# Two feed-forward layers after pooled attention: pairs of tiles 384 to 512 columns wide, first V remainders pooled on VectorE, and a new plan

## The chip, the cores and the metric

The kernel runs on one core of a Trainium2 chip. The metric is device time in microseconds (us) of one execution, the median of several. Engines are named as in the profile: PE multiplies matrices (TensorE), DVE is VectorE, ACT is ScalarE, POOL is GpSimd, and SP issues the DMA transfers.

## The reference

Attention over keys and values that are averaged in groups of 8, for 8 batches of 8 heads with 576 positions and 64 dimensions; then two feed-forward layers, 512 to 2048 to 512, over the 4608 tokens. All in float32.

```python
k_p = k.reshape(B, H, Sp, pool, D).mean(axis=3)      # 576 -> 72 positions
v_p = v.reshape(B, H, Sp, pool, D).mean(axis=3)
scores = scale * np.matmul(q, k_p.transpose(0, 1, 3, 2))
attn = softmax(scores)
x = np.matmul(attn, v_p)                             # then heads side by side: 4608 x 512
h = x @ moe_w_in;  x = np.maximum(0.01 * h, h) @ moe_w_out
h = x @ moe2_w_in; x = h * np.clip(h + 3.0, 0.0, 6.0) / 6.0 @ moe2_w_out
```

## The kernel before, in words

**Precision.** Each float32 operand of a large product is split into a high part in the matmul type (`float32r`) and the rest, and three products are summed (high x high, high x rest, rest x high). So each tile needs an ACT copy (the high part) and a DVE subtraction (the rest) before PE can use it.

**Attention** is done in 24 units (8 batches, three units each: two with 384 positions of four heads, one with the remaining 192 of all eight). `prep_k` and `prep_v` pool K and V; `scores`, `transposes`, `transpose_rem` and `values` follow. 72 pooled positions are kept as 64, the main part, and 8, the remainder. In the first batch, units 0 and 1 have V pooled by PE: `pool_v` (L427) multiplies eight slices by the identity into PSUM, once for the main part (128x128) and once for the remainder (32x64). Later units pool V by `sum_pool` (L405), a DVE reduction. DVE then multiplies the remainder by a mask (L486).

**The first 896 tokens** go through the first layer as plain tiles: 384 tokens with half of the hidden columns, then 512 tokens, then the 384 again with the other half (`moe_tile`; multiplications at L898 to L900 and L942 to L944). While these run, weights are loaded, decoded and split by ACT and DVE, and sums of weight blocks are stored in DRAM (`left`).

**Pairs.** The other 3712 tokens of the first layer (class `Pair1`) and all 4608 of the second (class `Pair`) go through as pairs of two tiles of n columns: four pairs, then five. A pair replaces the eight block products of a 2 x 2 product by seven (Strassen's scheme), in `first` and in `second`. `prepare` loads the pair's tokens (`xt`), forms the seven sums and splits them. Each pair streams all seven products' weights from `left` by SP's queue: 56 parts of 512 KB or fewer of 1 MB. Per pair `first` and `second` issue 336 multiplications each, all from `left_right` (L1163), whatever n is. n was 464, but 448 in the first pair of the second layer.

**The order of the work.** `C` holds slots at which attention units (`att`, `gaps`), weight sums (`left1`, `left2`, `when1`) and the next pair's preparation (`prep`, `prep2`) are recorded between the steps of the layers. The class `Plan` takes all recorded tasks with their dependencies and a price for each (`pe_cost`, `act_cost`, `dve_cost`, bytes over a rate), places them in time on every engine by list scheduling in 12 rounds, and the instructions are issued in that order, each engine first in, first out. Copies recorded early may go to ACT or DVE, as the planner finds. `Plan.order` also puts small multiplications of zeros (the fills, L1659) into PE's order where PE is planned to wait before the first layer's second multiplication begins, and twelve of them in a stretch of short multiplications and transposes (`weak`).

Of the kernel before, what the change touches and what calls it, by code (L numbers as in the profile page):

```python
# [10 lines left out]
F32 = mybir.dt.float32  # L11
# [8 lines left out]
B, H, S, D = 8, 8, 576, 64  # L20
DM, DFF = 512, 2048
POOL, SP = 8, 72
# [5 lines left out]
WIDTH = 464  # L28
STARTS = [0, T0, *range(T0 + T1, B * S + 1, WIDTH)]

# [3 lines left out]
    soon={0: 0, 1: 0, 2: 2000},  # L34
# [5 lines left out]
    when0=[0, 1, 0, 2, 5, 3, 10],  # L40
    att0=[0, 4, 8],
    gaps0=[0, 0, 2, 2, 0],
    when1=[4, 10, 20, 26],
    att1=[0, 7, 14, 22],
    gaps1=[0, 3, 3, 3, 0],
    att2=[0, 5],
    gaps2=[0, 1, 5, 6, 0],
    prep2=[26, 68],
    att=[[4, 26, 42, 51], [10, 24, 39, 58, 70], [0, 21, 40, 55], []],
    gaps=[[0, 7, 7, 11, 2], [0, 11, 9, 19, 1], [0, 2, 10, 11, 6], [7, 14, 2, 4, 4]],  # L50
    prep=[[85, 106], [94, 89], [102, 89], [84, 93]],
    left1=[[(0, 65)], [(1, 0), (2, 1), (3, 16)]],
    left2=[[], [], [(0, 40)], [(1, 23), (2, 45)], [(3, 18), (4, 39)], [(5, 23), (6, 40)], [(7, 15)]],
# [5 lines left out]
FIRST_LOADS = 1.35  # L59
WARM_FROM = 2700  # L60
# [47 lines left out]
class Plan:  # L108
# [102 lines left out]
    def order(self):  # L211
# [28 lines left out]
        out, busy, weak = [], WARM_FROM, 0.0  # L240
        for i in sorted(range(n), key=lambda i: (self.starts[i], i)):
            engine, cost, emit = self.chosen[i]
            if engine == "pe" and busy is not None:
                gap = self.starts[i] - busy
                out += [self.fill] * (int((gap - 200) / 56) + (6 if gap > 300 and busy > 12000 else 0))
# [13 lines left out]
def attention_moe_moe(ctx: ExitStack, tc: tile.TileContext, qt, kt, vm, vr, wt, wq, eye, mask, out):  # L259
# [42 lines left out]
    def pe_cost(n):  # L302
        return max(0.4435 * n + 5, 111)
# [124 lines left out]
    def pool_v(u):  # L428

        ps = buf("h", [128, 512], F32, 2, psum)  # L430
        u.vs, u.rs = ps("v", lambda t: t[:, 0:128]), ps("r", lambda t: t[:32, 128:192])
        for src, dst, n in ((u.v, u.vs, 128), (u.r, u.rs, 64)):

            def emit(src=src, dst=dst, n=n):
                for i in range(POOL):
                    PE.matmul(
                        out=dst.ap(),
                        lhsT=ident.ap()[: dst.ap().shape[0], : dst.ap().shape[0]],
                        rhs=src.ap()[:, i * n : i * n + n],
                        start=i == 0,  # L440
                        stop=i == POOL - 1,
                    )

            on_pe(1740 if n == 128 else 1320, emit, [src, ident], [dst], n < 128)
# [19 lines left out]
    def prep_v(u):  # L464
# [3 lines left out]
        if u.early:  # L468
            pool_v(u)
        else:  # L470
            sum_pool(u.vs, u.v, 128)
            sum_pool(u.rs, u.r, 64)
# [1157 lines left out]
    n = 11  # L1630
# [82 lines left out]
```

## Time and profile before

| | us |
|---|---|
| median of 3 runs | 1557.65 |
| the three runs | 1557.65, 1560.13, 1549.45 |
| the profiled execution | 1553.07 |
| its span, first to last instruction | 1551.3 |

The profile's page gives each engine's busy time in the span; the views of the trace split it by stretch (windows), by instruction in order of time (timeline), by what an engine waited for (waits), and by the chain of work that ended last. Times in the views are counted from the span's start. The granted clock is TensorE's, where 1.00 is 2.4 GHz and 0.50 is 1.2 GHz. The two halves of the first pair begin at 236.2 and 316.8 us, the following pairs at 391.2, 552.1 and 709.2, the second layer's at 849.8 us.

### The profile page before, as it was taken

The page shows a single profiled execution, that of the slowest core. Times are in us where ns is not written, and L with a number is a line of the kernel's source. Part 1 is how long each engine was busy: PE and PEld are TensorE (multiplying, and loading weights), DVE is VectorE, ACT ScalarE, POOL GpSimd, SP SyncE. Part 2 cuts the span into 40 slices and gives each one's busy share as a digit, 9 for nine tenths or more (in the row PEclk, how much of TensorE's full clock was granted, in tenths as well). Part 3 has the DMA queues.
Part 4 walks back from the last instruction along what each step waited for, and adds up shares of the span by engine and source line. Part 5 has one row for each costly group of instructions (what it writes and reads, how often), then busy time and mean ns, then how long its engine had stood idle before and what let it go on. Part 6 is the DMA issues. An engine that isn't in the chain of part 4 may idle for free.

```text
span 1551.3 us, 23074 instructions
## 1 busy us (share of the span) xinstructions
PE 1543.8 (100%) x7905; PEld 1381.0 (89%) x7905; DVE 1195.2 (77%) x2124; ACT 997.9 (64%) x2267; POOL 2.9 (0%) x14
## 2 busy tenths in 40 slices
PE   9999999999999999999999999999999999999999
PEld 7988898899989888888888999988888888888888
DVE  7999998599769876897597769559756946885494
ACT  5988767767777677766666656455555644664454
POOL 0000000000000000000000000000000000000000
PEclk9999999999999999999999999999999999999999
DMA  7999779998999899999997987766866775676664
GB/s 265 342 366 324 265 279 347 323 311 302 327 325 332 269 312 331 307 327 324 326 342 257 343 277 251 264 208 226 289 218 216 254 252 206 228 259 222 213 234 145
DMA packets 141140, 434.65 MB, mean 280 GB/s; under 512 B 14432, under 2 KB 56032, under 8 KB 122848
## 3 DMA queue, kind: packets, MB, share of 16 engines
q1 hardware_dynamic: 141024, 433.18, 80.7%
q8 instruction: 63, 1.03, 0.3%
q14 instruction: 53, 0.43, 0.1%
HBM read 345.57 MB, written 87.56 MB: 279 GB/s over the span
## 4 chain that ended last, share of the span: by engine, by line
PE 87%; DVE 7%; ACT 3%; DMA 1%; issue 1%; SPq 0%; ACTq 0%; DVEq 0%
PE y L1163 42%; PE h L1163 23%; PE a L1163 13%; PE a L715 2%; DVE raw L1028 2%; PE a L520 1%; DVE gl L329 1%; DVE st L329 1%; DMA xh<-x 1%; DVE w L1028 1%; PE h L898 1%; PE h L900 1%; PE h L899 1%; ACT s L604 1%; PE a L664 1%
## 5 line engine op out<-in xcount | busy, mean ns | idle before, releaser
L1028 DVE TENSOR_TENSOR w<-y,w 128x464 f32<-128x464 f32 (+1 forms) x124 | 79.2, 639 | 116.7 <-PE y L1163 113.5
L322 ACT ACTIVATE gh<-w 128x464 fp32r<-128x464 f32 (+1 forms) x140 | 82.5, 590 | 65.4 <-PE y L1163 31.1
L1163 PE MATMUL y<-w,xh 128*128 128x464 f32 (+1 forms) x552 | 122.8, 372 | 0.0
L1028 DVE TENSOR_TENSOR w<-w 128x464 f32<-128x464 f32 (+1 forms) x184 | 113.6, 639 | 3.2 <-ACT w L916 2.8
L1163 PEld LDWEIGHTS y<-w,xh 128*128 128x128 f32 x552 | 103.2, 188 | 11.2
L1361 DVE SCALAR_TENSOR_TENSOR gl<-w,gh 128x464 fp32r<-128x464 f32 (+1 forms) x140 | 89.0, 639 | 22.9 <-ACT gh L322 22.7
L319 ACT CAST gh<-w 128x464 fp32r<-128x464 f32 x128 | 74.3, 582 | 43.8 <-PE y L1163 22.2
L329 DVE TENSOR_TENSOR gl<-w,gh 128x464 fp32r<-128x464 f32 x128 | 81.6, 641 | 14.7 <-ACT gh L319 14.2
L1163 PE MATMUL y<-w,xl 128*128 128x464 f32 (+1 forms) x408 | 91.7, 373 | 0.0
L1332 ACT ACTIVATE gh<-w,three 128x464 f32<-128x464 f32 (+1 forms) x60 | 40.9, 681 | 69.8 <-DVE w L1028 69.8
L1163 PEld LDWEIGHTS y<-w,xl 128*128 128x128 f32 x408 | 76.1, 188 | 8.4
L1028 DVE TENSOR_TENSOR w<-h,w 128x464 f32<-128x464 f32 (+1 forms) x52 | 33.3, 640 | 62.7 <-PE h L1163 62.5
L916 ACT ACTIVATE w<-w 128x464 f32<-128x464 f32 x96 | 57.1, 601 | 36.5 <-DVE w L1028 35.5
L319 ACT COPY w<-y 128x464 f32<-128x464 f32 (+2 forms) x105 | 57.0, 546 | 32.4 <-PE y L1163 31.6
L329 DVE TENSOR_TENSOR st<-raw,st 128x512 fp32r<-128x512 f32 x88 | 60.4, 688 | 18.5 <-ACT st L319 18.2
L329 DVE TENSOR_TENSOR w<-x,w 128x464 fp32r<-128x464 f32 (+1 forms) x96 | 60.2, 639 | 11.6 <-ACT w L319 11.6
L1163 PE MATMUL y<-gh,raw 128*128 128x464 f32 (+1 forms) x224 | 69.1, 369 | 0.0
L1163 PE MATMUL h<-w,xl 128*128 128x464 f32 (+1 forms) x300 | 67.8, 373 | 0.0
L604 ACT ACTIVATE s<-a,mx 128x72 f32<-128x72 f32 x204 | 62.2, 339 | 7.4 <-DVE mx L580 7.1
L1163 PE MATMUL y<-w,w 128*128 128x464 f32 x288 | 64.4, 373 | 0.0
L1163 PE MATMUL h<-w,xh 128*128 128x464 f32 (+1 forms) x288 | 64.4, 372 | 0.0
L322 ACT ACTIVATE sb<-w 128x464 fp32r<-128x464 f32 (+1 forms) x70 | 41.3, 590 | 34.4 <-PE y L1163 16.6
(296 smaller groups left out, 4264.8 us busy)
## 6 DMA issues: line engine op xcount, KB each, us to landing
raw<-left SPq DMA_DIRECT2D x60, 1024.0 KB, 4.9
xl<-left SPq DMA_DIRECT2D x90, 512.0 KB, 5.3
left<-st SPq DMA_DIRECT2D x176, 256.0 KB, 5.5
xh<-left SPq DMA_DIRECT2D x86, 512.0 KB, 5.7
w<-left SPq DMA_DIRECT2D x74, 512.0 KB, 5.6
xh<-left SPq DMA_DIRECT2D x33, 1024.0 KB, 4.8
xl<-left SPq DMA_DIRECT2D x25, 1024.0 KB, 4.9
raw<-wq SPq DMA_DIRECT2D x16, 1024.0 KB, 7.5
```

What stands on the lines that cost most here:

```text
L319: a = lambda: ACT.copy(out=dst.ap(), in_=src.ap())
L322: a = lambda: ACT.mul(out=dst.ap(), in_=src.ap(), mul=scale)
L329: lambda: DVE.tensor_tensor(out=dst.ap(), in0=a.ap(), in1=f32(b.ap()), op=ALU.subtract),
L520: PE.matmul(out=to.get()[:, 2 * SP * i : 2 * SP * i + 2 * SP], lhsT=u.q.ap()[:, pi * HALF + CQ * c : pi * HALF + CQ * c + CQ], rhs=keys[u. ...
L604: ACT.activation(out=at()[:, c, h, :], in_=ps.get()[:, o : o + SP], func=AF.Exp, bias=mx.get()[:, c, h : h + 1], accum_out=sm.get()[:, 4 * ...
L664: PE.transpose(out=placed(u, ps.get(), c), in_=u.p(c, pi), identity=ident.ap())
L715: PE.matmul(out=ps.get()[:, c0 : c0 + n], lhsT=l(), rhs=r.ap()[:, c0 : c0 + n], start=i == 0, stop=i == len(ops) - 1)
L916: lambda: ACT.activation(out=dst.ap(), in_=src.ap(), func=AF.Prelu, alpha=0.01),
L1028: on_dve(n, lambda: DVE.tensor_tensor(out=dst.ap(), in0=a.ap(), in1=b.ap(), op=op), [a, b], [dst])
L1163: PE.matmul(out=o, lhsT=l, rhs=r, start=first and i == m == 0, stop=last and i == len(left) - 1 and m == 2, skip_group_check=True,)
L1332: lambda: ACT.activation(out=r.ap(), in_=h.ap(), func=AF.Relu, bias=three.ap()),
L1361: lambda: DVE.scalar_tensor_tensor(out=lo.ap(), in0=v.ap(), scalar=1.0 / 6.0, in1=f32(hi.ap()), op0=ALU.mult, op1=ALU.subtract),
```

## The change

- **Widths.** `WIDTHS1` and `WIDTHS2` replace one width: the first layer's four pairs are 384, 512, 448, 512 wide, the second layer's five are 512, 512, 512, 384, 384. Where a pair's columns come from two tiles of the layer before, `load_x` issues one transfer for each.
- **V remainders.** `pool_v` keeps only the main part on PE; the remainder of units 0 and 1 is reduced by DVE like all others, and the host lays it out for that.
- **Prices of the plan.** `pe_cost` is n/2.4 + 14 ns for multiples of 128, else + 16; the first loads count 1.08 instead of 1.35 of their bytes, the first weight loads 1.4; the fills at the start are counted from 980 ns at 107 ns each, later ones at 56, in gaps less 100 ns instead of 200.
- **Slots.** Nearly all slots of `C` are new, and the second layer's preparation has a pair of its own (`prep3`, 66 and 109 instead of 80 and 96). The count of operations per unit and per pair stays.

```diff
-WIDTH = 464
-STARTS = [0, T0, *range(T0 + T1, B * S + 1, WIDTH)]
+WIDTHS1 = [384, 512, 448, 512]
+WIDTHS2 = [512, 512, 512, 384, 384]
+STARTS = [0, T0, *(T0 + T1 + sum(WIDTHS1[: i // 2]) * 2 + (WIDTHS1[i // 2] if i % 2 else 0) for i in range(8)), B * S]
...
-    soon={0: 0, 1: 0, 2: 2000},
+    soon={0: 0, 1: 0, 2: 2000, 4: 0, 3: 0, 5: 0},
...
-    att=[[4, 26, 42, 51], [10, 24, 39, 58, 70], [0, 21, 40, 55], []],
+    att=[[4, 26, 33, 50], [10, 24, 39, 58, 75], [0, 21, 46, 58], []],
...
-FIRST_LOADS = 1.35
-WARM_FROM = 2700
+FIRST_LOADS = 1.08
+FIRST_WEIGHTS = 1.4
+WARM_FROM = 980
...
-                out += [self.fill] * (int((gap - 200) / 56) + (6 if gap > 300 and busy > 12000 else 0))
+                out += [self.fill] * (int((gap - 100) / (56 if out_of_rest else 107)) + (6 if gap > 300 and busy > 12000 else 0))
+                out_of_rest = True
...
     def pe_cost(n):
-        return max(0.4435 * n + 5, 111)
+        return max(n / 2.4 + (14 if n % 128 == 0 else 16), 111)
...
     def pool_v(u):
-        ps = buf("h", [128, 512], F32, 2, psum)
-        u.vs, u.rs = ps("v", lambda t: t[:, 0:128]), ps("r", lambda t: t[:32, 128:192])
-        for src, dst, n in ((u.v, u.vs, 128), (u.r, u.rs, 64)):
...
-            on_pe(1740 if n == 128 else 1320, emit, [src, ident], [dst], n < 128)
+        u.vs = buf("h", [128, 512], F32, 2, psum)(None, lambda t: t[:, 0:128])
...
+        on_pe(1800, emit, [u.v, ident], [u.vs])
...
             pool_v(u)
         else:
             sum_pool(u.vs, u.v, 128)
-            sum_pool(u.rs, u.r, 64)
+        sum_pool(u.rs, u.r, 64)
...
-    widths = [448] + [WIDTH] * 4
-    pairs1 = [Pair1(T0 + T1 + 2 * WIDTH * i, WIDTH) for i in range(4)]
-    pairs = [Pair(2 * sum(widths[:i]), n) for i, n in enumerate(widths)]
+    pairs1 = [Pair1(STARTS[2 + 2 * i], n) for i, n in enumerate(WIDTHS1)]
+    pairs = [Pair(2 * sum(WIDTHS2[:i]), n) for i, n in enumerate(WIDTHS2)]
...
-        prepare_pair(p.jobs, nxt, (80, 96))
+        prepare_pair(p.jobs, nxt, C["prep3"])
```

What this does to the order of instructions is shown at three places; lines below 1000 move by up to four. In PE's order the fills of the opening were 57 at the start and then groups of 17, 2, 9, 1, 12, 12 and 19; they are 41 and then 13, 13, 18, 12, 19, 12, 2, 12, 17 and 20. Before, only the last group stood behind the first multiplication with weights; now the last four do.

VectorE in the opening, from the second half of unit 1's key pooling to the mask of unit 0's V remainder. Before (`h_230` is PE's PSUM tile of pooled V):

```order
L409 TENSOR_REDUCE w_1_96<-w_1_96 128x72
L589 TENSOR_TENSOR sb_244<-y_1_207,mx_219 128x3x144
L615 TENSOR_SCALAR inv_248<-sm_211 128x12
L616 RECIPROCAL inv_248<-inv_248 128x12
L622 TENSOR_TENSOR rn_257<-s_198,inv_248 128x96
L638 TENSOR_TENSOR s_198<-s_198,inv_248 128x768
L580 TENSOR_REDUCE mx_219<-y_1_253 128x3x2
L486 TENSOR_TENSOR w_1_103<-h_230,mask_240 32x256
```

The same stretch of VectorE after (`raw_157` holds the loaded V of unit 0):

```order
L413 TENSOR_REDUCE w_1_96<-w_1_96 128x72
L594 TENSOR_REDUCE sm_203<-s_177 128x3x2
L327 TENSOR_SCALAR keys_1_79<-w_1_96 64x72 x2
L578 TENSOR_REDUCE mx_217<-y_1_198 128x3x2
L613 TENSOR_SCALAR inv_246<-sm_203 128x12
L413 TENSOR_REDUCE raw_157<-raw_157 32x64
L614 RECIPROCAL inv_246<-inv_246 128x12
L587 TENSOR_TENSOR sb_252<-y_1_198,mx_217 128x3x144
L620 TENSOR_TENSOR rn_254<-s_177,inv_246 128x96
L484 TENSOR_TENSOR w_1_149<-raw_157,mask_210 32x256
```

The reduction of the remainder (32x64) now stands in VectorE's queue, the mask reads its result instead of PSUM, and the scaling of `s` and the last maximum come behind the mask; the scaled keys of unit 1's second half are VectorE's too.

PE where the first layer begins, before (`h_342` is pooled V of unit 1, `h_434` the first product with weights, `y_3` the values of unit 1):

```order
L436 MATMUL h_342<-w_1_294,ident_168 32x64 x8
L898 MATMUL h_434<-xh_324,w_1_327 128x384
L899 MATMUL h_434<-xl_329,w_1_327 128x384
L900 MATMUL h_434<-xh_324,w_1_327 128x384
L898 MATMUL h_434<-xh_324,w_1_327 128x384
L899 MATMUL h_434<-xl_329,w_1_327 128x384
L900 MATMUL h_434<-xh_324,w_1_327 128x384
L715 MATMUL y_3_446<-w_1_83 128x384
```

The same place of PE after:

```order
L662 MATMUL y_2_409<-ident_153,sb_252 128x128 x3
L662 MATMUL y_2_416<-ident_153,sb_252 128x128 x3
L896 MATMUL h_421<-xh_333,w_1_341 128x384
L897 MATMUL h_421<-xl_339,w_1_341 128x384
L898 MATMUL h_421<-xh_333,w_1_341 128x384
L896 MATMUL h_421<-xh_333,w_1_341 128x384
L897 MATMUL h_421<-xl_339,w_1_341 128x384
L898 MATMUL h_421<-xh_333,w_1_341 128x384
L713 MATMUL y_3_433<-w_1_84 128x384
```

The pooling of the remainder is gone from PE, and the transposes of unit 1 (`y_2`), which stood ahead of the third unit's scores, now stand behind them.

SP's queue in the opening, before (`w_1_294` is V of unit 1; `w_1_242`, `w_1_259`, `w_1_278`, `w_2_419` and `w_2_456` are weights; `w_2_456` takes the buffer that held `w_1_294`):

```order
L797 DMA w_1_278<-wt 128x1024
L336 DMA w_1_294<-vm 128x1024
L336 DMA w_1_103<-qt 128x768
L797 DMA w_1_242<-wt 128x1024
L336 DMA w_1_294<-vr 32x512
L336 DMA raw_354<-kt 128x1152
L797 DMA w_1_278<-wt 128x1024
L336 DMA raw_397<-vr 32x512
L797 DMA w_2_419<-wt 128x1024
L797 DMA w_1_259<-wt 128x1024
L797 DMA w_2_456<-wt 128x1024 x2
```

SP's queue after (`w_1_262` is V of unit 1, and `w_2_444` takes its buffer):

```order
L340 DMA w_1_262<-vm 128x1024
L340 DMA w_1_262<-vr 32x512
L795 DMA w_1_297<-wt 128x1024
L340 DMA w_1_149<-qt 128x768
L795 DMA w_1_212<-wt 128x1024
L340 DMA raw_358<-kt 128x1152
L795 DMA w_1_297<-wt 128x1024
L795 DMA w_2_414<-wt 128x1024
L795 DMA w_2_444<-wt 128x1024
L340 DMA raw_450<-vr 32x512
```

V of unit 1 is loaded one weight transfer earlier, its remainder right behind it, and the first transfer into its buffer stands ahead of two of those that it stood behind.

## Rows read from the trace of the kernel before

**Rows 1.** The page's busy times: us, share of the span, instructions, by engine.
```profile
PE 1543.8 (100%) x7905; PEld 1381.0 (89%) x7905; DVE 1195.2 (77%) x2124; ACT 997.9 (64%) x2267; POOL 2.9 (0%) x14
```
**Rows 2.** PE's waits: what it waited for, us in total, times, longest.
```profile
PE a L715 <- DVE w L320: 1.2, 1, 1.2
...
PE a L664 <- DVE s L638: 0.4, 1, 0.4
PE a L715 <- ACT tr L319: 0.3, 1, 0.3
```
**Rows 3.** Windows: stretch, length, busy us by engine, granted clock, DMA share, GB/s.
```profile
60.00:140.00 80.00, 79.93 (x430) 68.22 (x429) 78.76 (x151) 68.26 (x202) 0.00 (x0) 1.00 1.01 358
...
236.20:391.20 155.00, 155.00 (x801) 139.13 (x800) 125.14 (x225) 110.12 (x281) 0.40 (x2) 1.00 0.93 319
391.20:552.10 160.90, 160.90 (x867) 144.71 (x865) 129.62 (x233) 117.17 (x315) 0.00 (x0) 1.00 0.93 315
552.10:709.20 157.10, 156.60 (x820) 139.80 (x814) 126.94 (x230) 116.58 (x304) 0.00 (x0) 1.00 0.93 317
709.20:849.80 140.60, 140.60 (x674) 126.01 (x673) 104.81 (x180) 89.73 (x165) 0.00 (x0) 1.00 0.91 316
```
**Rows 4.** The chain that ended last, in the pairs: start us, us, what.
```profile
339.81 10.03 PE h L1163 x48
...
947.21 9.73 PE a L1163 x48
```
**Rows 5.** PE's timeline in the plain tiles: start us, us, instruction.
```profile
50.11 0.33 PE L942 MATMUL y<-gh,w 128*128 128x384 f32 x1
...
58.26 0.34 PE L944 MATMUL y<-gh,w 128*128 128x384 f32 x1
...
127.83 0.39 PE L898 MATMUL h<-xh,w 128*128 128x512 f32 x1
...
134.41 0.39 PE L900 MATMUL h<-xh,w 128*128 128x512 f32 x1
```
**Rows 6.** VectorE's groups by shape: count, busy us, mean ns, idle before.
```profile
L1028 DVE TENSOR_TENSOR w<-y,w 128x464 f32<-128x464 f32 x112 | 71.7, 640 | 101.6 <-PE y L1163 98.4 <-ACT w L916 1.3 <-ACT gh L1332 1.0
...
L409 DVE TENSOR_REDUCE raw<-raw 32x64 f32<-32x512 f32 x14 | 9.3, 666 | 0.0
...
L329 DVE TENSOR_TENSOR gl<-u,gh 128x384 fp32r<-128x384 f32 x16 | 8.8, 551 | 0.4 <-ACT gh L319 0.4
```
**Rows 7.** The chain that ended last, in the opening.
```profile
0.98 5.95 PE idle L1659 x57
...
14.01 1.80 PE h L436 x16
...
18.33 4.77 PE a L715 x8
...
23.85 3.32 PE h L436 x16
...
30.07 1.00 PE h L436 x16
...
32.32 3.16 PE y L715 x8
...
36.73 1.07 PE idle L1659 x19
...
42.03 3.96 PE a L715 x16
```
**Rows 8.** ScalarE's timeline in the opening.
```profile
4.39 0.26 ACT L322 ACTIVATE keys<-raw 64x72 f32<-64x72 f32 x1 [2.16 <-DVE raw L409]
```
**Rows 9.** Windows of PE alone: stretch, length, busy us, granted clock, DMA share, GB/s.
```profile
18.00:20.00 2.00, 1.67 (x5) 1.00 1.04 404
...
21.00:26.00 5.00, 5.00 (x18) 0.50 0.65 245
```
**Rows 10.** SP's timeline in the opening.
```profile
16.69 15.22 SPq L797 DMA_DIRECT2D w<-wt  x4
```

More of the change, by code (lines that the diff above doesn't have):

```diff
@@ L39 @@
     parts=31,
-    when0=[0, 1, 0, 2, 5, 3, 10],
+    when0=[0, 0, 2, 0, 4, 0, 5],
     att0=[0, 4, 8],
[L42 to L45, printed above, removed]
+    gaps0=[0, 0, 2, 2, 4],
+    when1=[4, 8, 21, 26],
+    att1=[0, 4, 14, 22],
+    gaps1=[0, 3, 0, 3, 1],
     att2=[0, 5],
-    gaps2=[0, 1, 5, 6, 0],
-    prep2=[26, 68],
-    att=[[4, 26, 42, 51], [10, 24, 39, 58, 70], [0, 21, 40, 55], []],
[L50 to L53, printed above, removed]
+    gaps2=[0, 1, 5, 6, 3],
+    prep2=[33, 72],
+    att=[[4, 26, 33, 50], [10, 24, 39, 58, 75], [0, 21, 46, 58], []],
+    gaps=[[0, 6, 7, 11, 0], [0, 11, 9, 16, 3], [0, 0, 10, 11, 13], [29, 25, 3, 2, 32]],
+    prep3=[66, 109],
+    prep=[[82, 93], [98, 118], [95, 94], [98, 81]],
+    left1=[[[0, 66]], [[1, 14], [2, 6], [3, 19]]],
+    left2=[[], [], [[0, 32]], [[1, 42], [2, 41]], [[3, 16], [4, 37]], [[5, 9], [6, 42]], [[7, 5]]],
 )
@@ L239, in order @@
         self.idle = []
-        out, busy, weak = [], WARM_FROM, 0.0
+        out, busy, weak, out_of_rest = [], WARM_FROM, 0.0, False
         for i in sorted(range(n), key=lambda i: (self.starts[i], i)):
@@ L428, in pool_v, with emit @@
     def pool_v(u):
-        ps = buf("h", [128, 512], F32, 2, psum)
-        u.vs, u.rs = ps("v", lambda t: t[:, 0:128]), ps("r", lambda t: t[:32, 128:192])
-        for src, dst, n in ((u.v, u.vs, 128), (u.r, u.rs, 64)):
[L434 to L442, printed above, removed]
-            on_pe(1740 if n == 128 else 1320, emit, [src, ident], [dst], n < 128)
+        u.vs = buf("h", [128, 512], F32, 2, psum)(None, lambda t: t[:, 0:128])
+        def emit():
+            for i in range(POOL):
+                PE.matmul(
+                    out=u.vs.ap(), lhsT=ident.ap(), rhs=u.v.ap()[:, i * 128 : i * 128 + 128], start=i == 0, stop=i == POOL - 1
+                )
+        on_pe(1800, emit, [u.v, ident], [u.vs])
     held_keys, held_values, whole_v, whole_r = {}, {}, {}, {}
@@ L795, in load_w @@
             on_dma(
-                1 << 20 if h is None else 1 << 19,
+                (1 << 20 if h is None else 1 << 19) * (FIRST_WEIGHTS if f == 0 else 1),
                 lambda dst=dst, cut=cut: DMA.dma_start(out=dst.ap().bitcast(I32), in_=cut(wt[ORDER[f]].bitcast(I32))),
@@ L1687 @@
     vm, vr = c(vm).reshape(B, 2, 128, 128, POOL), vr.reshape(B, 2, 32, D, POOL)
-    vm[0], vr[0] = [a[0].swapaxes(2, 3).reshape(a[0].shape) for a in (vm, vr)]
+    vm[0] = vm[0].swapaxes(2, 3).reshape(vm[0].shape)
     wi = moe_w_in.reshape(4, 128, NF, 128).transpose(2, 1, 0, 3).reshape(NF, 128, 512)
```

## The prediction

> **What bounds the kernel now.** I read the page's busy times first, then PE's waits, then one window per stage, then the chain of waits in the opening, then the timeline for the spacing of matrix multiplications. PE is busy for 1543.8 us of a 1551.3 us span [rows 1], and the view of waits has next to nothing after the opening: five waits before 31 us, in sum 2.4, the longest of 1.2; the third row here stands for three of 0.2 to 0.3 us [rows 2]. The windows say where other engines come close: VectorE is busy 78.76 of 80 us from 60 to 140 us, but PE has no gap there; in the four pairs of the first feed-forward layer (236.2 to 849.8 us) PE has no gap worth 1 us either, with the DMA engines at a share of 0.91 to 0.93 [rows 3]. So from about 31 us on the end is set by the sum of PE's multiplications, and before that by a chain through several engines. Only two things can shorten the kernel much: fewer ns per column in the long part, and a shorter opening.
>
> **Widths: a term of the long part.** Each of the nine pairs issues 336 multiplications in `first` and 336 in `second`, whatever its width; the tokens per layer stay 3712 and 4608. So the number of multiplications and of columns is the same, and what can differ is the time that a multiplication takes above its columns at 2.4 GHz. The chain gives 10.03 us for 48 of 464 columns (208.96 ns, 15.6 above 464/2.4) and 9.73 for 48 of 448 (202.7 ns, 16.0 above) [rows 4]. The other two widths run in the earlier tiles. At 384 the multiplication that starts at 58.26 is the 47th after the one at 50.11: 8.15/47 = 173.4 ns, 13.4 above 160. At 512, from 127.83 to 134.41 in 29 steps: 226.9 ns, 13.6 above 213.3 [rows 5]. Before, eight pairs are 464 wide and one 448; after, three are 384, five 512, one 448. Leaving out the 448 (672 x 202.7 both times): before 5376 x 0.20896 = 1123.4 us; after 2016 x 0.1734 + 3360 x 0.2269 = 349.6 + 762.4 = 1112.0. **Term: -11.4 us.** It lies wholly on the path, because PE is the bound there. The bounds: with the overheads of all widths equal it is 0; with a reading error of 0.01 us over 29 steps it is 1.2 us more or less.
>
> The Trainium skill's page TensorE: Matmul & The Clock Gate, section "Wait — 56ns, not 53.3ns?", puts the excess of a back-to-back multiplication at a fixed 2.5 ns, whatever its width. By that rule this term is 0, as count and columns stay; by the rows it is -11.4, and the rows decide, since they show 13 to 16 ns and a difference between widths.
>
> **The narrow pairs.** A 384-wide pair takes PE 672 x 0.1734 = 116.5 us instead of 140.4, but streams the same weights (29.4 MB). I added the bytes in SP's order from one pair's first weight stream to the next one's: before 47.6, 50.2, 50.6, 44.6 MB in the four pairs of the first layer, now 42.9, 54.2, 49.4, 46.5 MB, so the new slots take work out of the narrow first pair. The attention inside these stages is what the window is longer than 140.4 us: 14.6, 20.5, 16.7 and 0.2 us [rows 3]. New stage lengths: 131.1, 173.0, 152.9, 152.7 us, needing 327, 313, 323, 304 GB/s. The windows show 315 to 319 GB/s in these stages without a wait of PE, and 358 GB/s over 80 us from 60 to 140 us [rows 3]; so 327 is between what was given here and what was given at most. If 319 were the limit, the first pair would wait 42.9/0.319 - 131.1 = 3.4 us; if 358, 0. The nearest row by kind is the 319, but with its share at 0.93 it is not at its end; I take **+0.5 us**, bounds 0 and 3.4. VectorE: an operation of 464 columns takes 640 ns and one of 384 takes 551 [rows 6], a ratio of 0.86 against PE's 0.83. The fourth pair (without attention) has 104.8 us of VectorE, the first 125.1 [rows 3]; 104.8 x 0.86 + 20.3 = 110 of 131.1 us, so VectorE still hides behind PE; without that cover each operation more would cost 0.55 us. The last two 384-wide pairs have no attention and no weight preparation, and I cost them, the moved preparation slots, `soon` and the planner's new prices at nothing: they only order what lies beside PE's unbroken row of multiplications, and a slip would show as single waits of 0.2 to 0.8 us.
>
> **The opening.** I count what PE does up to the values of the third attention unit (42.03 in the chain) beside its real work.
> - Fills at the start (by the order of both programs): 57 take 5.95 us, 0.104 each [rows 7], and after only 41 stand there: -1.7 us. ScalarE's half of the first keys was done at 4.65 [rows 8], before the 41 fills can end (5.3); if the queries land later than that, part is waited for instead: bounds -1.7 and -0.5.
> - V remainders: PE's eight instructions of 32x64 take 1.00 us at 30.07 in the chain [rows 7]; the other eight run in a stretch padded with fills and cost nothing. VectorE gets two reductions of 0.67 us [rows 6], into a queue on which the first values wait. Term -1.0, bounds -2.0 and +0.3.
> - The clock: it was granted 0.50 from about 20 to 27 us, after a stretch (18 to 20) in which PE was busy 1.67 of 2 us [rows 9]. Eight multiplications of values took 4.77 us there and 3.16 at 32.32; sixteen of the V pooling took 3.32 and before 1.80 [rows 7]: 1.61 + 1.52 = 3.1 us lost. After, 12 and 19 fills stand around the transposes ahead of the values. Term -3.1, bounds -3.1 and 0.
> - Other fills: 72 before, 138 after, up to the point where PE runs unbroken; 19 take 1.07 us [rows 7], so 66 x 0.056 = +3.7. They stand where PE would wait, and the five waits of 2.4 us should mostly go [rows 2]: +1.3, bounds 0 and +3.7.
>
> Together **-4.5 us**; all ends to one side -6.8 and +3.5. What is late next: VectorE's queue, which I find filled from 7 us on.
>
> **Sum.** -11.4 + 0.5 - 4.5 = -15.4 us. The profiled execution took 1553.07 us, so 1537.7 by it. It lies 4.6 below the median of the three runs, which range over 10.7 us; the mean of these four executions is 1555.1, and from it I get 1539.7: I say **1540**. A measurement of this kernel can tell about 1%, 15.6 us, from no change; the forecast sits at that edge.
>
> **Rivals.**
> - A, the time above the columns doesn't depend on the width where a pair runs (the differences seen are those of other tiles: other weights, other buffers). Then the widths give 0 and the rest -4.0: 1551. For it: 384 and 512 were never run in a pair. Against: 448 and 464, both in pairs, agree with each other at 16, and the two multiples of 128 agree at 13.5 in two different tiles.
> - B, the clock falls again in the opening, as fills don't make it certain: -12.3, so 1543. For it: transposes and short multiplications still fill that stretch, and VectorE still ends the waits.
> - C, the slower one: the weight stream. SP's queue is first in, first out, and if the DMA engines give no more than a fixed rate in the first layer's pairs, every stage takes its bytes over that rate. At 310 GB/s the waits are 7.2, 1.9, 6.3 and 0, in sum 15.4: all is eaten; below, the kernel is slower than before. At 300 GB/s: 11.8 + 7.7 + 11.6 + 2.2 = 33.3 us, so -15.9 + 33.3 = +17.4: 1572. Against: 315 to 319 GB/s was given without one wait.
> - D, the opening gives more, all terms at their good ends: -11.4 - 6.8 = -18.2, so 1537. For it: four weight loads stood in SP's queue from 16.69 to 31.9 [rows 10], the third and fourth of them behind a buffer that PE's remainder pooling freed last; now it is freed after the main pooling and VectorE's reduction. Against: from 60 to 140 us PE had no gap to lose [rows 3].
>
> **How the numbers follow.** Forecast 0.50, A 0.08, B 0.22, C 0.05, D 0.15. Faster by over 1%: half of the forecast, most of D, a little of B (run-to-run spread): 0.43. Slower by over 1%: the worse half of C: 0.03. Within: 0.54. Range: D with the runs' spread below gives 1530; A with it, and C up to break-even, gives 1553.
>
> **What would show it.** Right: 48 multiplications of 512 and 384 columns in a pair take 10.89 and 8.32 us in the chain; PE's waits stay below 1 us each after 60 us; the granted clock stays at 1.00 from 15 to 30 us; the first values start near 16 to 17 us instead of 18.33 and those of the third unit near 37 instead of 42.03. Wrong: 512 at 229 ns or more (A); 0.50 in the opening (B); PE waiting for tiles streamed from `left` in the first 384-wide pair, or the DMA share at 1.0 through it (C); new fills between weights multiplications that PE had no need of.

## The result and the profile after

| | before | after |
|---|---|---|
| median, us | 1557.33 (6 runs, 1549.45 to 1560.13) | 1542.51 (6 runs, 1541.80 to 1544.41) |
| the profiled execution | 1553.07 | 1541.80 |
| its span | 1551.3 | 1540.0 |
| start of the first pair | 236.2 | 231.9 |
| from there to PE's last multiplication | 1311.0 | 1304.3 |

The ratio after to before is 0.9916, with a 95% interval of 0.9889 to 0.9943. The prediction said 1540 (1530 to 1553). The two profiled executions differ by 11.3 us of span: 4.3 up to the first pair, 6.7 in the nine pairs, 0.3 behind them.

Busy times of the page of the kernel after, which answer to [rows 1]:

```profile
PE 1529.5 (99%) x7923; PEld 1351.7 (88%) x7923; DVE 1196.0 (78%) x2123; ACT 997.2 (65%) x2270; POOL 2.9 (0%) x14
```

PE is busy 14.3 us less in a span that is 11.3 shorter: 3 us more of it are idle. The view of PE's waits in the kernel after (what it waited for, us in total, times, longest) shows where; it answers to [rows 2]:

```profile
PE a L662 <- DVE s L636: 2.1, 1, 2.1
...
PE y L941 <- DVE gl L333: 0.8, 1, 0.8
PE h L1161 <- ACT gh L323: 0.7, 1, 0.7
PE a L518 <- DMA q<-qt: 0.5, 1, 0.5
PE y L1161 <- DMA xh<-left: 0.5, 1, 0.5
PE h L1161 <- DVE gl L333: 0.4, 1, 0.4
```

Only at the place of the second row, near 230 us, did the kernel before wait too (0.3 us); the other five are new at their places. The largest is for the softmax scaling of the fifth attention unit (L636), at 67 us.

**The pairs.** The windows of the five stretches (four pairs of the first layer, then the second layer), with the instructions of `left_right` alone: stretch, length, PE's and its weight loads' busy us (count), granted clock, DMA share, GB/s. First before, then after:

```profile
236.20:391.20 155.00, 144.76 (x672) 125.36 (x673) 1.00 0.93 319
391.20:552.10 160.90, 146.27 (x674) 124.74 (x672) 1.00 0.93 315
552.10:709.20 157.10, 145.09 (x673) 124.77 (x674) 1.00 0.93 317
709.20:849.80 140.60, 140.60 (x674) 126.01 (x673) 1.00 0.91 316
849.80:1547.20 697.40, 697.40 (x3360) 630.80 (x3359) 1.00 0.69 240
sum 1311.00, PE 1274.11 PEld 1131.67; mean PE 254.82 PEld 226.33
```

```profile
231.90:364.40 132.50, 120.83 (x672) 116.21 (x673) 1.00 0.95 334
364.40:540.70 176.30, 159.21 (x675) 124.61 (x673) 1.00 0.90 316
540.70:692.30 151.60, 140.78 (x672) 125.12 (x673) 1.00 0.92 321
692.30:844.70 152.40, 152.40 (x674) 126.20 (x674) 1.00 0.90 304
844.70:1536.20 691.50, 690.62 (x3361) 610.93 (x3359) 1.00 0.70 241
sum 1304.30, PE 1263.84 PEld 1103.08; mean PE 252.77 PEld 220.62
```

The same number of multiplications takes 1274.11 us before and 1263.84 after: -10.3. The first, 384-wide stage got 334 GB/s, more than any of the four before. Multiplications of other tiles fill the rest of each stage; PE's busy time over all instructions is 1310.50 of 1311.0 us before and 1301.98 of 1304.3 after, so the other work in the pairs grew from 36.4 to 38.1 us, and the idle time from 0.5 to 2.3.

The growth of 1.7 us is no new work. One attention unit's last stage on PE (six transposes, three of the remainder, twelve multiplications of values) stands from 230.1 to 236.2 us before, ahead of the first pair, and from 233.1 to 237.2 us after, behind the start of the first pair. The transposes by themselves (L664 before, L662 after) in the windows of the pairs, the same columns as above:

```profile
236.20:1547.20 1311.00, 10.16 (x72) 8.64 (x72) 1.00 0.80 276
...
231.90:1536.20 1304.30, 11.44 (x78) 9.60 (x78) 1.00 0.80 277
```

So 1.7 of the 4.3 us by which the first pair starts earlier are work that was moved behind its start; at equal work the opening won 2.6.

The spacing itself, from the chain of the kernel after (start us, us, what), beside [rows 4]:

```profile
330.21 8.32 PE y L1161 x48
...
653.56 9.73 PE y L1161 x48
```

8.32/48 is 173.3 ns for 384 columns, and 9.73/48 is 202.7 for 448. A pair of 512 in the second layer reads 10.88 for 48, 226.7 ns ("1259.99 10.88 PE a L1161 x48"). The spacings foretold from plain tiles hold in the pairs.

**The opening.** The chain of the kernel after, beside [rows 7]:

```profile
6.62 0.73 PE idle L1656 x13
...
16.25 3.22 PE a L713 x8
19.47 1.98 PE h L438 x16
...
25.74 3.16 PE y L713 x8
...
68.29 0.88 DVE s L636
69.17 0.14 issue
69.30 1.46 PE a L662 x6
70.76 0.32 PE h L896
```

The first values start at 16.25 instead of 18.33 and take 3.22 instead of 4.77; the second values start at 25.74 instead of 32.32; those of the third unit at 35.97 instead of 42.03. So 6.1 us were won by then; 2.6 are left at the first pair (4.3, less the 1.7 of work moved behind its start), so 3.5 were given back. The last four rows show where: PE waits until 69.17 for VectorE (2.1 us in the list of waits), and the multiplication behind it takes 0.32 us where 384 columns take 0.17. Windows of the kernel after, around that place (PE, weight loads, DVE, ACT, POOL busy; granted clock; DMA share; GB/s):

```profile
21.00:26.00 5.00, 5.00 (x66) 4.38 (x64) 4.57 (x9) 4.33 (x15) 0.00 (x0) 1.00 0.78 251
...
67.00:69.00 2.00, 0.24 (x2) 0.00 (x0) 2.00 (x6) 1.98 (x6) 0.00 (x0) 1.00 1.09 383
...
70.00:72.00 2.00, 2.00 (x9) 2.00 (x8) 1.97 (x4) 1.97 (x5) 0.00 (x0) 0.50 1.18 283
```

From 21 to 26 us, where [rows 9] had 0.50, the clock is granted in full. PE then idles for most of 67 to 69 while VectorE and ScalarE are busy throughout, and from 70 to 72 the clock is 0.50.

### The profile page after: what moved, and what is told of

Its sections match the earlier page's. It is cut to its first block, busy times and chain, and to the rows that moved or that the text cites. A ratio compares the mean times of both kernels' runs of the same rounds, so it can differ in the third digit from the quotient of the medians.

```text
span 1540.0 us, 23125 instructions
## 1 busy us (share of the span) xinstructions
PE 1529.5 (99%) x7923; PEld 1351.7 (88%) x7923; DVE 1196.0 (78%) x2123; ACT 997.2 (65%) x2270; POOL 2.9 (0%) x14
## 4 chain that ended last, share of the span: by engine, by line
PE 89%; DVE 5%; ACT 3%; DMA 2%; issue 1%; SPq 0%; DVEq 0%; ACTq 0%
PE y L1161 43%; PE h L1161 23%; PE a L1161 12%; PE a L713 2%; DVE raw L1026 1%; PE a L518 1%; PE a L662 1%; PE h L896 1%; PE h L898 1%; PE h L897 1%; DMA left<-st 1%; PE a L535 1%; PE y L941 1%; PE y L940 1%; PE y L942 1%
## 5 line engine op out<-in xcount | busy, mean ns | idle before, releaser
L1026 DVE TENSOR_TENSOR w<-y,w 128x512 f32<-128x512 f32 (+2 forms) x124 | 78.6, 636 | 113.0 <-PE y L1161 112.2
L326 ACT ACTIVATE gh<-w 128x512 fp32r<-128x512 f32 (+1 forms) x140 | 82.1, 589 | 63.4 <-PE y L1161 25.1
L1161 PE MATMUL y<-w,xh 128*128 128x512 f32 (+2 forms) x552 | 122.0, 370 | 0.5 <-DMA xh<-left 0.5
L1026 DVE TENSOR_TENSOR w<-w 128x512 f32<-128x512 f32 (+2 forms) x184 | 112.3, 630 | 3.0 <-ACT w L914 2.6
L1161 PEld LDWEIGHTS y<-w,xh 128*128 128x128 f32 x552 | 100.6, 188 | 13.4 <-ACT gh L1330 0.9
L323 ACT CAST gh<-w 128x512 fp32r<-128x512 f32 (+2 forms) x128 | 74.6, 584 | 49.7 <-PE y L1161 28.1
L1359 DVE SCALAR_TENSOR_TENSOR gl<-w,gh 128x512 fp32r<-128x512 f32 (+1 forms) x140 | 88.1, 631 | 19.0 <-ACT gh L326 18.9
L333 DVE TENSOR_TENSOR gl<-w,gh 128x512 fp32r<-128x512 f32 (+2 forms) x128 | 81.2, 636 | 21.0 <-ACT gh L323 20.6
L1161 PE MATMUL y<-w,xl 128*128 128x512 f32 (+2 forms) x408 | 91.2, 371 | 0.0
L1161 PEld LDWEIGHTS y<-w,xl 128*128 128x128 f32 x408 | 74.6, 188 | 10.0 <-DVE st L1026 0.3
L1161 PE MATMUL y<-gh,raw 128*128 128x512 f32 (+1 forms) x224 | 69.2, 369 | 0.0
L1161 PE MATMUL h<-w,xl 128*128 128x512 f32 (+2 forms) x300 | 66.6, 369 | 0.0
L323 ACT CAST w<-x 128x512 fp32r<-128x512 f32 (+2 forms) x96 | 55.1, 584 | 14.3 <-DVE x L1026 7.9
L1161 PE MATMUL h<-w,xh 128*128 128x512 f32 (+2 forms) x288 | 64.3, 371 | 0.0
L1161 PE MATMUL y<-w,w 128*128 128x512 f32 (+2 forms) x288 | 64.1, 372 | 0.0
```

The source lines that it names most:

```text
L323: a = lambda: ACT.copy(out=dst.ap(), in_=src.ap())
L326: a = lambda: ACT.mul(out=dst.ap(), in_=src.ap(), mul=scale)
L333: lambda: DVE.tensor_tensor(out=dst.ap(), in0=a.ap(), in1=f32(b.ap()), op=ALU.subtract),
L1026: on_dve(n, lambda: DVE.tensor_tensor(out=dst.ap(), in0=a.ap(), in1=b.ap(), op=op), [a, b], [dst])
L1161: PE.matmul(out=o, lhsT=l, rhs=r, start=first and i == m == 0, stop=last and i == len(left) - 1 and m == 2, skip_group_check=True,)
L1359: lambda: DVE.scalar_tensor_tensor(out=lo.ap(), in0=v.ap(), scalar=1.0 / 6.0, in1=f32(hi.ap()), op0=ALU.mult, op1=ALU.subtract),
```

## The experiments

Times of later sets are compared with the kernel before on the same chip. The third column is the start of the first pair, the fourth the sum of `left_right`'s multiplications in the pairs as in the windows above, the fifth the length of the pairs; all three are of the profiled execution. The start of the first pair is not the same point of the work in every kernel: behind it stand 460 of PE's attention instructions in before, e3 and e6, 481 (1.4 to 1.8 us more) in after, e1, e4, e7, e8, e9 and e11, and 448 (1.2 to 1.6 us less) in e2 and e12.

| kernel | median (runs) | first pair | multiplications | pairs | ratio to before, 95% interval |
|---|---|---|---|---|---|
| before | 1557.33 (6) | 236.2 | 1274.11 | 1311.0 | |
| after | 1542.51 (6) | 231.9 | 1263.84 | 1304.3 | 0.9889 to 0.9943 |
| e1 widths only | 1550.12 (11) | 240.5 | 1264.73 | 1304.1 | 0.9976 to 0.9996 |
| e2 old widths | 1555.71 (11) | 237.9 | 1277.68 | 1312.8 | 1.0011 to 1.0036 |
| e3 before again | 1553.97 (12) | 233.3 | 1273.30 | 1310.2 | 0.9991 to 1.0018 |
| e4 fills at the wait | 1540.32 (4) | 230.8 | 1264.72 | 1305.2 | 0.9902 to 0.9932 |
| e6 fills only | 1554.20 (12) | 233.8 | 1279.87 | 1317.1 | 0.9991 to 1.0023 |
| e7 remainders on PE | 1545.80 (10) | 233.1 | 1264.99 | 1306.7 | 0.9933 to 0.9972 |
| e8 after again | 1541.19 (6) | 231.2 | 1264.65 | 1304.4 | 0.9905 to 0.9956 |
| e9 no 448 | 1547.30 (11) | 234.3 | 1266.07 | 1308.6 | 0.9966 to 0.9985 |
| e11 fills again | 1542.20 (5) | 230.9 | 1264.57 | 1305.7 | 0.9930 to 0.9959 |
| e12 remainders only | 1553.70 (12) | 234.6 | 1273.06 | 1310.1 | 0.9998 to 1.0030 |

e1 to e4 ran on one chip, where the kernel before took 1552.17 us (29 runs); e5 to e8 on a second, 1552.45 (21 runs); e9 to e11 on a third, 1550.78 (15 runs); e12 on the chip of the first set, 1552.53 (17 runs). Across these sets the kernel before ranges from 1547.67 to 1560.43.

### e1 and e2: the widths without the rest, and the rest without the widths

```diff
 e1: the kernel before with
-WIDTH = 464
+WIDTHS1 = [384, 512, 448, 512]
+WIDTHS2 = [512, 512, 512, 384, 384]
 e2: the kernel after with
-WIDTHS1 = [384, 512, 448, 512]
-WIDTHS2 = [512, 512, 512, 384, 384]
+WIDTHS1 = [464] * 4
+WIDTHS2 = [448] + [464] * 4
```

> The kernel before with the new widths alone: its slots, prices, fills and PE pooling of the V remainders stay. Theory (the time above the columns falls with the widths, and the slots matter little): 48 multiplications of 512 and 384 columns take 10.88 and 8.32 us; the nine pairs last about 1302 us instead of 1311, and the kernel is 8 to 11 us faster than before. Rival (the new widths pay only with the new slots): the spacing is the same, but PE waits in the first 384-wide pair, where the old slots leave 47.6 MB to stream in about 131 us, for 5 us or more, and the kernel gains under 5 us. Rival A of the prediction (nothing gained by widths): no difference from before.

> The changed kernel with the old widths (464, and 448 in the second layer's first pair); all else stays as changed. Theory (opening and widths add up): the first pair still starts near 232 us, the second layer's pairs last 697 us as before, and the kernel is 3.5 to 6.5 us faster than before. Rival (most of the gain is the opening, as the runs of before spread over 10 us and those after over 3): 9 us or more faster, with runs as close together as those of the changed kernel.

In e1 the multiplications take 1264.73 us, 9.4 less than before, and the pairs 1304.1: the widths give nearly the same with the old slots. But the first pair starts at 240.5. PE's waits of e1 tell why:

```profile
PE a L716 <- DVE s L590: 2.8, 1, 2.8
PE h L1164 <- DVE sb L330: 1.1, 1, 1.1
PE a L665 <- ACT vrm L320: 1.0, 1, 1.0
```

The wait of 2.8 us stands near 211 us, in the part that the widths do not touch, and the granted clock is 0.50 from 216 to 218 us, after it. In e2 a wait of 3.4 us stands just ahead of the first pair. The planner orders all tasks at once, so other widths reorder the opening too. So the two halves of the change, each without the other, do not add up to it (medians 2.1 us below and 3.5 above the kernel before on that chip): the widths and the rest belong together. Which part of the rest matters, the slots or the prices, no run tells: neither was run alone. e2 also brought something not foretold. Its multiplications take 3.6 us longer than those of the kernel before, at the same widths. Its chain in the second layer:

```profile
1057.19 10.08 PE h L1161 x48
```

That is 210.0 ns for 464 columns, where [rows 4] had 209.0. The longer spacing stands in the trace of the kernel before too, in its second pair, the one behind the row that the prediction read:

```profile
521.75 28.98 PE y L1163 x138
```

28.98/138 is 210.0 ns. In its fourth pair the steps go from 208.9 to 210.0 at 817.4 us, behind one step of 240 ns, in a stage in which PE is busy 140.60 of 140.60 us.

### e3: the kernel before once more

No edit.

> The kernel before once more, for the span and granted clock of each of its runs. If the clock explains the spread of 10 us, the runs with more time have a lower mean clock: 0.001 of mean clock is about 3.1 us at half speed, so 1.5 us of work lost, and 10 us of spread would need clocks from about 0.999 down to 0.992. Rival (the spread comes from something else, as the landing of transfers or the start of the program): the mean clocks stay within 0.002 of each other and do not follow the times.

In this execution the clock did not fall in the opening. Its windows over the stretches of [rows 9], all engines:

```profile
18.00:20.00 2.00, 1.95 (x5) 0.89 (x6) 2.00 (x5) 0.89 (x3) 0.00 (x0) 1.00 1.03 408
21.00:26.00 5.00, 5.00 (x64) 4.28 (x63) 4.85 (x10) 4.73 (x11) 0.00 (x0) 1.00 0.68 248
```

The third unit's values start at 38.53 instead of 42.03, and the first pair at 233.3 instead of 236.2: the fall costs 3.5 us at the first place and 2.9 at the second. The prediction's 3.1 was right in size, but it is not in every execution of the kernel before. The runs of e3 at a mean clock of 1.00 fall into two groups of spans, 1547.2 to 1547.8 and 1553.1 to 1553.3, three runs each. A cause other than the clock is worth 5.6 us. The mean clocks of all twelve runs lie within 0.002 of each other and do not follow the times, as the rival said.

### e6: the new fills alone, in the kernel before

```diff
-WARM_FROM = 2700
+WARM_FROM = 980
...
-                out += [self.fill] * (int((gap - 200) / 56) + (6 if gap > 300 and busy > 12000 else 0))
+                out += [self.fill] * (int((gap - 100) / (56 if out_of_rest else 107)) + (6 if gap > 300 and busy > 12000 else 0))
+                out_of_rest = True
```

> The kernel before with the change's rule for the fills alone. Theory (the fills hold the clock, and the clock is about 3 us of the opening): the granted clock stays at 1.00 through the opening in every run, the first pair begins at 231 to 233.5 us instead of 236.2, and the median is 1.5 to 3.5 us below the kernel before; what is left of the spread is the 464-wide spacing, some 5.5 us between two groups of runs. Rival (the fills cost on PE's path what they save): the first pair at 235 or later, and the median within 1 us of the kernel before.

The profiled execution keeps the clock at 1.00 in the opening. Its third unit's values start at 38.75 and its first pair at 233.8, as in e3 (38.53, 233.3). So where the clock holds anyway, the fills win nothing: what they take off the start is waited for instead. The median says the same (ratio 1.0007). Nor do they hold the clock in every run, which was expected of them: two of the 12 have a mean clock of 0.998, against eight of 21 of the kernel before at 0.997 or 0.998 on this chip. The other ten still span 1548.1 to 1556.1 us. The profiled one is near the upper end (1554.9), and the row of its second layer (`left_right` alone, as above) shows where it spends the time:

```profile
847.80:1550.90 703.10, 703.10 (x3360) 629.89 (x3359) 1.00 0.68 238
```

The same instructions take 703.10 us here and 697.40 in both executions of the kernel before that were profiled: +5.7, all of it spacing. Its chain shows it for 448 (9.92 for 48, 206.7 ns, instead of 9.73) and for 464 (10.08):

```profile
947.12 9.92 PE a L1164 x48
...
1510.96 10.08 PE a L1164 x48
```

### e5 and e10: the spacing by itself

The kernel has nothing but blocks of multiplications, and leaves the whole computation out.

```python
for i, n in enumerate(WIDTHS):
    ps = psum.tile([128, 512], F32, name=f"ps{i}", tag="ps", bufs=2)
    for j in range(96):
        PE.matmul(out=ps[:, 0:n], lhsT=w[:, j % 8, :], rhs=x[:, j % 2, 0:n], start=j == 0, stop=j == 95)
```

> A kernel that leaves the whole computation out: 96 back-to-back multiplications of 128x128 by each of 13 widths (256 to 512 columns, 464 and 512 twice), with no other engine at work between a width's first and last. Theory (the time above the columns belongs to the width): at full clock 512 and 384 again take 226.9 and 173.4 ns from start to start, 448 202.7, and 464 209 to 210, so 13 to 14 above n/2.4 for multiples of 128 and 15.5 to 16.5 for the others; 480, 416 and 496 lie with the others. Rival (it belongs to the neighbours, that is to VectorE's and ScalarE's reads of PSUM or the weight stream in the pairs): all widths have the same time above n/2.4 here, within 0.5 ns. On the two spacings of 464 (208.96 and 210.0): if they belong to the width alone, its two blocks here show one of them, and single spacings of about 205 and 215 in turn when it is the longer; if to the neighbours, neither.

> A kernel that leaves the whole computation out: 22 blocks of 96 back-to-back multiplications, 464 columns after 512, 464, 256, 416 and 384, and 448 likewise. Theory (a spacing is set where a run of one width begins, and kept as long as it runs unbroken): every block of 464 shows 208.9 or 210.0 throughout, and every block of 448 202.7 or 206.7; two blocks of 464 that follow each other share one. If the width ahead decides, equal neighbours give equal spacings; if it is chance, they don't. Rival (it changes within a run): block means lie between the two. 512, 384 and 416 take 226.7, 173.3 and 186.7 wherever they stand.

In e5, 464 took 210.0 ns in the block behind 512 and 208.9 in the one behind 256, and 448 took 206.6. In e10 each block keeps one spacing, and the width ahead decides which. Timeline of e10, two rows for each block (start us, us, instruction, count in the window; the second row holds the window's last multiplications, so that the steps between the two starts are the first count less the second):

```profile
21.23 18.52 PE L35 MATMUL ps<-x,w 128*128 128x512 f32 x81
38.91 0.84 PE L35 MATMUL ps<-x,w 128*128 128x512 f32 x3
43.08 16.75 PE L35 MATMUL ps<-x,w 128*128 128x464 f32 x79
59.04 0.79 PE L35 MATMUL ps<-x,w 128*128 128x464 f32 x3
94.91 16.66 PE L35 MATMUL ps<-x,w 128*128 128x464 f32 x79
110.78 0.79 PE L35 MATMUL ps<-x,w 128*128 128x464 f32 x3
273.82 15.97 PE L35 MATMUL ps<-x,w 128*128 128x448 f32 x78
288.81 0.97 PE L35 MATMUL ps<-x,w 128*128 128x448 f32 x4
397.71 16.90 PE L35 MATMUL ps<-x,w 128*128 128x448 f32 x81
413.83 0.78 PE L35 MATMUL ps<-x,w 128*128 128x448 f32 x3
```

512: 17.68/78 = 226.7 ns. 464: 15.96/76 = 210.0 behind 512, 15.87/76 = 208.8 behind 256. 448: 14.99/74 = 202.6 behind 512, 16.12/78 = 206.7 behind 384. The other blocks follow suit: 464 is 210.0 behind 416 and 384 too, and a block of 464 behind one of 464 keeps the latter's spacing; 448 is 202.7 behind 512, 448, 256 and 416. 416 takes 186.7 behind 464 but 188.3 behind 448, against the expectation of one spacing. Blocks of 512 (226.7) and 384 (173.3) show one spacing each wherever they stand. With no other engine at work, the time above n/2.4 still differs between widths, and the rival of e5 (the neighbours) falls. But e5's theory of two classes failed too: 416 and 496 took 13.3 ns above n/2.4 there, like the multiples of 128, and 480 took 16.7.

The width ahead does not settle it in the large kernel. In the second layer of both the kernel before and e2, 464 follows 448 at 202.7 ns, and takes 208.9 in the one and 210.0 in the other.

### e4 and e11: fills ahead of the fifth unit's transposes

```diff
+                if at_wait and pi == 0:
+                    for _ in range(34):
+                        PE.matmul(out=ps.get()[:, 0:128], lhsT=plan.zeros, rhs=plan.zeros, start=True, stop=True)
                 for c in range(NC):
                     PE.transpose(out=placed(u, ps.get(), c), in_=u.p(c, pi), identity=ident.ap())
```

`at_wait` is true for the fifth unit alone.

> The changed kernel with 34 multiplications of zeros ahead of the transposes of the fifth attention unit, where PE waited for 2.1 us (67.2 to 69.3) and then ran at half clock for 3.4 us. Theory (the wait costs twice, itself and the clock): the granted clock stays at 1.00 from 60 to 80 us, the first pair starts at about 230 instead of 231.9 us, and the kernel is 1 to 2 us faster than the changed one. Rival (the work behind the wait is late by VectorE and ScalarE, so that PE's speed there buys nothing): the clock stays up, but the first pair starts at 231.5 us or later.

> The kernel after with fills ahead of the fifth unit's transposes once more, on the chip of this set. If it is faster than the kernel after by itself: 1539.5 to 1541 here, with a clock of 1.00. If the fills gave nothing and the chips differed: 1541 to 1543.

The wait of 2.1 us is gone from PE's list, as the fills stand in its place, the clock is 1.00 in all nine runs, and the first pair starts at 230.8 and 230.9. Of the twelve runs of the kernel after, three have 1.00. The medians are 1540.32 and 1542.20 against 1542.51 and 1541.19 of the kernel after in its two sets. The two kernels did not run in the same set; their intervals against the kernel before overlap, so no difference is shown. A reason stands in e8.

### e8: the kernel after once more

No edit.

> The kernel after once more, on the same chip as the others of this set. Theory (a wait of 2.1 us at 67 us, then a clock fall): 1541 to 1543.5, runs within 4 us of each other, and the two that do and don't show a clock below 1.00 differ by 1.5 to 2.5; 1.5 to 2.5 us above the kernel with fills ahead of that wait. Rival (the fills there changed nothing, chips differ): within 0.5 us of it, 1540 to 1541.

The wait at 67 us is there again with its 2.1 us, but the clock stays up behind it. The windows of e8:

```profile
67.00:69.00 2.00, 0.29 (x2) 0.00 (x0) 2.00 (x6) 1.98 (x6) 0.00 (x0) 1.00 1.09 383
...
70.00:72.00 2.00, 2.00 (x14) 2.00 (x13) 1.97 (x5) 1.97 (x5) 0.00 (x0) 1.00 1.16 287
```

Fourteen multiplications run from 70 to 72 us instead of nine, and the one that starts at 72.80 in the profiled execution after starts at 71.32 here: the half clock cost 1.5 us there. The first pair starts at 231.2, only 0.7 earlier; the rest is given back by then, among others at waits for VectorE's `gl` and ScalarE's `gh`, 0.6 longer in sum. So the fills save the clock only in executions in which it would fall, and the wait itself they cannot save. That the wait costs twice holds for one of two executions. On this chip the kernel after is 11.3 us below the kernel before (1541.19, 1552.45), less than the 14.8 of the first set.

### e7 and e12: the V remainders

e7 is the kernel after with `pool_v` as before; e12 is the kernel before with the new `pool_v` as its only edit.

```diff
 e12
             sum_pool(u.vs, u.v, 128)
-            sum_pool(u.rs, u.r, 64)
+        sum_pool(u.rs, u.r, 64)
```

> The kernel after, with the V remainders of units 0 and 1 pooled by PE again. The prediction's term says 1.0 us slower in the opening (first pair at 232.9 instead of 231.9), 2.0 at most. Rival (VectorE's queue, full from 7 us on, paid for the reductions): no slower, or up to 0.5 us faster. A third way, as the single parts so far went: the plan places other work elsewhere and a new wait before the pairs costs more than the term, 2 to 4 us, with a clock fall beside it.

> The kernel before with the one part that units 0 and 1 have their V remainders pooled by VectorE; fills, widths, slots and prices as before. The prediction's term: PE is rid of eight instructions of 1.0 us on the path, VectorE gets two reductions of 0.67 us; the first pair begins 1.0 us earlier than in an execution of the kernel before with the same clock (232.3 against 233.3 with the clock at 1.00, 235.2 against 236.2 with the fall at 20 us), bounds -2.0 and +0.3. Rival (a part alone makes the plan place other work elsewhere, as widths and slots alone did): a new wait of 1 to 4 us ahead of the first pair, which begins at 234 to 240, and a median 1 to 4 us above the kernel before.

Undone, the part costs 4.6 us (1545.80 against 1541.19 of e8); by itself it gains nothing (ratio 1.0014). In e7 the first pair starts 1.9 later than in e8, and the pairs take 2.3 longer, with `left_right`'s multiplications equal within 0.4. In e12 the clock is 1.00 throughout the opening, and its chain has the third unit's values at 36.39:

```profile
36.39 3.96 PE a L709 x16
```

That is 2.1 us before e3's 38.53, at equal clock: twice the term. But the first pair starts at 234.6, 1.3 later than in e3. Of this, 1.2 is work: twelve multiplications of scores stand ahead of its start here and behind it in e3. At equal work the two starts are within 0.1, so the 2.1 were lost again. PE's waits ahead of the first pair are others, and longer:

```profile
PE a L680 <- ACT th L319: 1.2, 1, 1.2
...
PE y L938 <- DVE w L329: 0.8, 1, 0.8
```

From 31 to 84 us PE is busy for 50.66 of 53 us in e12 and for 52.92 in e3. So the gain is there where the part acts (the plan around it changed too), and waits lose it again some 30 us later, as in the kernel after.

### e9: no width with two spacings

e4's kernel with

```diff
-WIDTHS1 = [384, 512, 448, 512]
+WIDTHS1 = [416, 512, 416, 512]
```

> The kernel after with fills ahead of the fifth unit's transposes, and the first layer's pairs 416, 512, 416, 512 wide instead of 384, 512, 448, 512, so that no width with two spacings is left. Theory (448 takes 202.7 or 206.7 ns, 416 a steady 186.7, 13.3 above its columns): 672 multiplications at 13.3 instead of 16.0 or 20.0 ns above their columns save 1.8 or 4.5 us, 1538 if the plan gives no new wait, and every run within 2 us. Rival (slots belong to widths, as the single parts of the change showed): the plan places work elsewhere and new waits of 2 to 4 us take it back, 1540 to 1544.

Neither came true: 1547.30 is above both ranges. 416 is not steady: the chain of e9 in its third pair,

```profile
673.05 9.04 PE h L1165 x48
```

gives 188.3 ns, the longer spacing that e10 showed behind 448. And the plan made new waits: 1.9 (ScalarE's `st`), 1.9 (the weights `xh` from `left`), 1.5 and 1.4 us. The first pair starts at 234.3, 3.5 later than in e4, though nothing ahead of it was edited.

## Why the prediction was right, point by point

- **The bound.** Right: beyond the opening the time is the sum of PE's multiplications.
- **Widths, -11.4.** Measured -10.3 between the profiled executions, -9.4 in e1. The spacings came out as read from the plain tiles (173.3, 226.7), so rival A falls. Of the missing 1.1 us, half is in the first layer (-3.5 of -4.0), where these multiplications alternate with attention: the second pair takes 159.21 us, 6.9 above 672 x 0.2267 (before: 146.27, 5.9 above 672 x 0.20896). The other half is in the second layer (-6.8 of -7.4), where the kernel before took 697.40 us, 0.5 less than its spacings read to 0.01 us gave. The rule of the Trainium skill (page TensorE: Matmul & The Clock Gate, section "Wait — 56ns, not 53.3ns?"), 2.5 ns whatever the width, would have given 0; the rows of e10, in `float32r`, disagree with it, at 13.3 to 20 ns. The fills, in bfloat16, come near it: 19 of 128 columns take 1.07 us [rows 7], 56.3 ns each, 3.0 above n/2.4.
- **The same term, unseen.** In the second layer the trace of before showed 464 at its shorter spacing throughout; the longer one, in its first layer, was not read. Executions with the longer one (e2 and e6, 1277.68 and 1279.87 us) are 3.6 and 5.8 us worse, so against these the widths give 13.8 and 16.0. This and the clock are large enough for the 14.8 between the first set's medians, where the profiled spans differ by 11.3; the other executions of that set have no trace. The sum gave 1537.7 and the profiled execution took 1541.80; the 2.3 us that the prediction added for the mean of four executions brought it to 1540, nearer than its terms were.
- **The narrow pairs, +0.5, and everything cost at nothing.** A step that failed, in size. The transfer side was right: 334 GB/s without a wait in the 384-wide first pair, so rival C falls. But "a slip would show as single waits of 0.2 to 0.8 us", cost at nothing, came to 1.8 us more idle time in the pairs (0.7 and 0.4 near 472 us, 0.5 near 850, others), 1.3 more than said. The other work in them grew by 1.7, which is the attention stage moved from ahead of the first pair. At 472 VectorE's queue was full: the rest of `gh` that PE wanted stood behind a pooling of 1.13 us and three sums of 0.6.
- **The opening, -4.5.** The larger failure, also in size: the first pair starts 4.3 earlier, but at equal work only 2.6. Up to the third unit's values 6.1 us were won. The clock is 3.5 of them (e3), near the term of 3.1. The V remainders are worth 2.1 (e12), the good end of their bounds, not 1.0. The start fills, -1.7 in the sum, are worth nothing alone (e6, with 47 instead of 41 at the start): in the kernel after the scores do start at 5.65 instead of 6.93, after 0.53 of waiting for the queries, but the chain comes through other engines before the third unit. The term for the other fills rests on a misreading: of the waits of 2.4 us that it lets go, only the 1.2 and one of 0.3 (with 0.2 of issue) stand ahead of 31 us; two of 0.3 stand between 225 and 236 us and the one of 0.4 in the third pair. By that the term would have been +2.0, not +1.3. The kernel then lost 3.6 at 67 us (2.1 of wait, 1.5 of half clock) to what the text asked, "what is late next": VectorE's queue, but far behind where I had looked. The sign "PE's waits stay below 1 us each after 60 us" did not hold. Rival B, a clock that falls again, is thus half true: at another place, for 1.5 us, and not in every execution.
- **Rival D** fell: what the opening won beyond 4.5 us was given back, and more.
- **The clock's term** was right only against executions of the kernel before in which the clock fell (e3 did not). Against e3, whose first pair starts at 233.3, the new opening is worth 1.4 to 2.1 us (231.9, 231.2), and with the 1.7 of moved work taken off, next to nothing. The spans say the same. In e3 and e8 the clock stays up; their spans are 1547.6 and 1539.4 us, 8.2 apart, and the multiplications of the pairs are 8.7 apart (1273.30, 1264.65). So against an execution of the kernel before in which the clock holds, the gain is the widths (one pair of executions, on two chips); the opening adds to it where the clock falls there.

The sum by terms: widths 1.1 short, the pairs' idle time 1.3 more, the opening 1.9 short, 0.3 gained behind the pairs: 4.0 us less than the 15.4 foretold, and the spans differ by 11.3, 4.1 less. That 1540 came so close to 1541.80 is in part luck: these shortfalls were offset by 2.3 us added for runs that the profiled execution does not stand for.

## What to carry to other kernels

Where PE is the bound, read the time between the starts of back-to-back multiplications for each width from the trace, and choose widths by it; a width may also have two spacings, so read it from several executions and stages before trusting the third digit. A plan that orders all engines at once makes parts of a change inseparable: judge them only together, and price the slips (here 1.8 us in the pairs and 3.6 at 67 us) instead of costing them at nothing. Before the start of a stage is compared between two such plans, count the work that stands ahead of it. A term that rests on a clock fall counts only in those executions in which it falls, so look at the clock of every run before taking it in full.

## What the runs showed of the hardware that was not expected

- Back-to-back multiplications of 128x128 by n columns at 2.4 GHz take 13.3 ns above n/2.4 for 512 and 384 in every unbroken stretch seen, but 464 takes 15.6 or 16.7, 448 16.0 or 20.0, and 416 13.3 or 15.0. In e10 the width ahead of a block decides which, and the block keeps it. In the large kernel one of them can hold for long (464 at 210.0 ns in e2's second layer, from 987 us to the end), and can change behind a single step of 240 ns (before, 817.4 us), which in e3 left it as it was (813.9 us). What sets it there was not found out.
- This is worth 5.7 us in the second layer alone, at a full clock (e6 against before and e3), and may be a large part of the spread of the kernel before (1547.67 to 1560.43). That it is, is not shown: no execution of that kernel with the longer spacing in its second layer was profiled. Eleven of the 12 runs of the kernel after, whose second layer has only 512 and 384, lie between 1539.35 and 1544.41 (one at 1548.12, with a mean clock of 0.996).
- The same wait of 2.1 us at the same place was followed by a half clock in one execution, from 69 to 73 us, and by a full one in another.
